# Finding the 24th candidate of a score row by folding sorted lists, for four tiles at once

## The chip, the cores and the metric

The kernel runs on one core of one Trainium2 chip. The metric is the device time of one execution in microseconds (us), median of three runs; the same program is profiled once more, and every instruction row below comes from that one profiled execution.

## The reference, cut to what matters

Top-32 attention, then a dense layer of three matmuls joined by a maximum, then a layer of eight experts of which each token goes to one. The part that the change touches is the attention (batch 4, 8 heads, 576 tokens, head size 64):

```
scores = scale * np.matmul(q, k.transpose(0, 1, 3, 2))
kth = np.partition(scores, -top_k, axis=-1)[..., -top_k:-top_k + 1]
mask = scores >= kth
scores = np.where(mask, scores, -1000000000.0)
scores = scores - np.max(scores, axis=-1, keepdims=True)
attn = np.exp(scores)
attn = attn / (np.sum(attn, axis=-1, keepdims=True) + 1e-09)
return np.matmul(attn, v).astype(np.float32)
```

Here `top_k` is 32. For every row of 576 scores the kernel must find the 32nd largest.

## The kernel before, in words

**Tiles.** The 4 x 8 x 576 rows of scores are cut into 144 tiles of 128 rows (`tiles`, `NTL`); a row has 576 scores. Four tiles in a row make a group (`G`), so there are 36 groups. The remainder of 64 rows of a head shares a tile with that of another head: four such "pair" tiles, one group, for each of the four batches.

**One loop of steps, a software pipeline.** The main loop counts steps `t`. In step `t` each stage works on the tile that lies its lag behind: scores of tile t+2 (TensorE), their copy out of PSUM for t+1 (`st_evac`, ScalarE), the search for tile t, and so on. The constants `L_...` are these lags. The order of the calls in the loop is the order of the instructions on each engine; there is no other scheduler. `bulk` is a list of VectorE pieces of the step and `tail_bulk` of pieces for its end; `run_bulk` issues them one by one and after each piece lets every open `chain` (a list of small instructions) issue one. Chains in `must` are issued to their end after `run_bulk`. `after(n, f)` puts work of other engines n steps later.

**The search, before.** `st_chunks` cuts the row of 576 into six pieces of 96 and takes the eight largest of each (MAX8 gives them sorted, largest first): 48 candidates. One step later `st_rounds` takes the eight largest of the 48, replaces them by a very low value (MATCH_REPLACE8, with a load of the eight values ahead of it), takes the next eight, replaces, and takes the third eight: the last of them is the 24th candidate. This is done for each tile by itself. `st_thr` (ScalarE) makes from it, tile by tile, the bound `bf`, and once a group the bias `be` of the later exponential from the largest value. `st_over` (ScalarE, lag 2) counts by the sign how many scores lie above the bound and marks them; `st_rest` (GpSimd, lag 3) subtracts the mark, which takes the marked ones out of the race; `st_next8` (VectorE, lag 4) takes the eight largest of what is left; `st_pick` makes a selector from the count, and `st_kth` (lag 8 of the group's first tile, ahead of the step's other VectorE work) picks the 32nd largest. From lag 9 on it is used: for two tiles of a group VectorE multiplies the exponential by a comparison (`st_mask`), for the other two ScalarE and GpSimd push the scores down ahead of the exponential (`st_gap`, `st_drop`). Then come splitting into two halves of 16 bit (`st_split`, `st_split2`), a transposing DMA (`st_ptr`) and the product with v (`st_av`), and `st_x` writes the group's result and turns it for the dense layer. `f` has two buffers (`NFB`), the marks `g` four (`NGB`).

**Other work in the same steps.** The matmuls of the dense layer and of the first experts run as units between the attention's (`run_units`), paced by a credit per step; weights are loaded and split into two halves of 16 bit (`prep_w`, `piece`). A last stretch without attention holds the rest of the experts.

**VectorE's PSUM bank.** One PSUM tile `vec` of 512 floats holds small operands of VectorE (`part` gives out pieces of it), among them the searches' results `vy8`.

**A second program.** `attempt(ctx, True)` is a slow exact version that runs only if the count `again` at the end says that the fast one missed a row; `general` marks its branches.

Of the kernel before, what the change touches and what calls it, by code (L numbers as in the profile page):

```python
# [12 lines left out]
ALU = mybir.AluOpType  # L13
# [6 lines left out]
def kernel(  # L20
# [74 lines left out]
    def attempt(ctx, general):  # L95
        const = ctx.enter_context(tc.tile_pool(name="const", bufs=1))
        iota32 = const.tile([P, G, 9], F32, name="iota32")
# [11 lines left out]
        NY8 = 3  # L109
# [12 lines left out]
        vy8 = [part(G * 9).rearrange("p (g e) -> p g e", g=G) for _ in range(NY8)]  # L122
        vt1 = [part(NE) for _ in range(3)]
# [7 lines left out]
        def consts():  # L131
# [8 lines left out]
            nc.vector.tensor_copy(out=viota, in_=iota32)  # L140
            nc.vector.tensor_copy(out=vrev, in_=rev8)
# [480 lines left out]
        with ExitStack() as p1:  # L622
# [26 lines left out]
            NPH, NHS = L_PTR - L_SPLIT + 1, 2  # L649
            phl = [a_p.tile([P, 2, SPAD], F16, name=f"phl{i}") for i in range(NPH)]  # L650
            if not general:

                hsel = a_p.tile([P, NHS, G, 9], F16, name="hsel")
                hkth = a_p.tile([P, NG, G], F32, name="hkth")
                heq = a_p.tile([P, NG, G, 1], F16, name="heq")
# [224 lines left out]
            Sps, Ss, T1, T3, zz, bf, be, cnt, y8, kth, ff, ee, pt = ({} for _ in range(13))  # L880
# [21 lines left out]
            cands, gg = {}, {}  # L902

            def st_chunks(n):
                if general:
                    return
                s = Ss[n]
                c = sm_p.tile([P, CAND * 8], F32, tag="c", name="c", bufs=2)
                cands[n] = c
                for j in range(0, CAND, 2):  # L910
                    def pair(j=j):
                        for i in (j, j + 1):
                            nc.vector.max(out=c[:, i * 8:(i + 1) * 8], in_=s[:, i * CW:(i + 1) * CW])  # L913
                    bulk.append(pair)

            def st_rounds(n):
                g, i = divmod(n, G)
                if i == 0:
                    T1[g] = sm_p.tile([P, G, 8], F32, tag="T1", name="T1", bufs=2)
                    if not general:  # L920
                        T3[g] = sm_p.tile([P, G, 8], F32, tag="T3", name="T3", bufs=2)
                if general:
                    return chain([lambda: nc.vector.max(out=T1[g][:, i], in_=Ss[n])])
                c = cands.pop(n)
                c2 = sm_p.tile([P, CAND * 8], F32, tag="c2", name="c2", bufs=1)
                t2 = sm_p.tile([P, 8], F32, tag="t2", name="t2", bufs=1)
# [9 lines left out]
            def st_bias(g):  # L936
                be[g] = sm_p.tile([P, G, 1], F32, tag="be", name="be")
                nc.scalar.activation(out=be[g], in_=T1[g][:, :, 0:1], func=ACTF.Copy, scale=-ESC)

            def st_thr(n):  # L940
                g, i = divmod(n, G)
                if general:
                    if i == G - 1:
                        st_bias(g)
                    return
                if i == 0:
                    cnt[g] = sm_p.tile([P, G, 1], F32, tag="cnt", name="cnt")
                    bf[g] = sm_p.tile([P, G, 1], F32, tag="bf", name="bf")
                nc.scalar.activation(out=bf[g][:, i], in_=T3[g][:, i, 7:8], func=ACTF.Copy, scale=-(1.0 - 2.0 ** -21))
                if i == G - 1:  # L950
                    st_bias(g)
# [15 lines left out]
            def st_next8(n):  # L967
# [3 lines left out]
                if i == 0:  # L971
                    y8[g] = vy8[g % NY8]
# [3 lines left out]
            def st_pick(g):  # L976
# [3 lines left out]
                bulk.append(lambda: nc.vector.tensor_tensor(out=hsel[:, g % NHS], in0=viota,  # L980
                                                            in1=cnt[g].to_broadcast([P, G, 9]), op=ALU.is_equal))
                tail_bulk.append(lambda: nc.vector.tensor_copy(out=y8[g][:, :, 0:1], in_=T3[g][:, :, 7:8]))
# [3 lines left out]
            def st_kth(g):  # L986
                kt = sm_p.tile([P, G], F32, tag="kth", name="kth") if general else hkth[:, g]
                kth[g] = kt
                if general:
# [13 lines left out]
                    lambda: nc.vector.tensor_tensor(out=y8[g], in0=hsel[:, g % NHS], in1=y8[g], op=ALU.mult),  # L1003
# [3 lines left out]
            def st_verdict():  # L1007

                hit = a_p.tile([P, NG * G], F16, name="hit")
# [71 lines left out]
            def st_x(g):  # L1081
# [6 lines left out]
                if first:  # L1088
# [3 lines left out]
                if kind == "pair":  # L1092
# [11 lines left out]
                def turn():  # L1104
# [4 lines left out]
                    else:  # L1109
                        if b % 2 == 0:  # L1110
                            xrem[b // 2] = m_ps[0].tile([P, 2, KD, 2 * REM], F16, tag="xR", name="xR", bufs=1)
                        xr = xrem[b // 2]
                        o = (b % 2) * REM
                        for i in range(2):
                            nc.sync.dma_start_transpose(
                                out=xr[:, i, :, o:o + REM],
                                in_=t[i * REM:(i + 1) * REM].rearrange("p e d -> p (e d)"),
                            )
                        if b % 2 == 1:
                            KH = KD // 2  # L1120
# [637 lines left out]
```

## Time and profile before

| what | us |
|---|---|
| median of 3 runs | 954.28 |
| lowest and highest | 954.03, 956.29 |
| the profiled execution, its own time | 951.46 |
| span of its instructions, first to last | 949.7 |
| VectorE (DVE) busy in it | 762.5 (80%) |
| TensorE (PE) busy | 751.6 (79%) |
| ScalarE (ACT) busy | 694.3 (73%) |
| GpSimd (POOL) busy | 608.6 (64%) |

A share of busy time is an average over the whole span. The attention lasts from about 23 us (the first copy of scores) to about 711 us (the last mask), and the engines' shares in it differ from those after it. The duration of an instruction in a row is from its start to its end; a following instruction of the same engine can start before that end, so what an instruction takes from its engine is better read from one start to the next.

### The profile page before, as it was taken

How to read it: one execution, taken by the hardware profiler on the slowest of the kernel's cores; microseconds unless marked ns; L12 is line 12 of the kernel's file. 1: busy time of each engine (PE TensorE's matmuls, PEld its weight loads, DVE VectorE, ACT ScalarE, POOL GpSimd, SP SyncE). 2: the span in 40 equal slices, each digit the busy share in tenths (PEclk: the TensorE clock that was granted, in tenths of full speed). 3: DMA queues.
4: the chain of work that ended last, by engine and by line, in shares of the span. 5: the costliest groups of instructions: out<-in, count | busy, mean ns of one | idle time of the engine just before them, and what ended most of it. 6: DMA issues, size and time to landing. Idle time of an engine off the chain costs nothing. (4 is left out here: it accounts for less than half of the span.)

```text
span 949.7 us, 29065 instructions
## 1 busy us (share of the span) xinstructions
PE 751.6 (79%) x10606; PEld 578.1 (61%) x10606; DVE 762.5 (80%) x3110; ACT 694.3 (73%) x1463; POOL 608.6 (64%) x552
## 2 busy tenths in 40 slices
PE   0212368888777899878898998889999999999992
PEld 0100237666555677657677787567887767588881
DVE  4999999999998999998998899788972335567671
ACT  2668899997898988898897997887863231466661
POOL 1457798998988789787877898687985221111110
PEclk9999999999998999899989999889999999999996
DMA  9681977775996788699969888687799358699270
GB/s 229 204 260 29 223 158 153 138 143 105 184 165 151 143 161 175 111 206 176 173 128 179 170 139 154 131 188 127 170 168 156 91 150 278 177 299 279 63 216 16
DMA packets 372164, 155.93 MB, mean 164 GB/s; under 512 B 331931, under 2 KB 348319, under 8 KB 372000
## 3 DMA queue, kind: packets, MB, share of 16 engines
q1 hardware_dynamic: 368128, 143.10, 71.9%
q0 software_dynamic: 3136, 9.46, 2.8%
q8 instruction: 87, 1.43, 0.6%
q10 hardware_dynamic: 736, 1.32, 0.5%
q14 instruction: 77, 0.63, 0.3%
HBM read 76.06 MB, written 16.67 MB: 98 GB/s over the span
## 5 line engine op out<-in xcount | busy, mean ns | idle before, releaser
L355 PEld LDWEIGHTS <-W 128*128 128x128 f16 x4560 | 248.2, 100 | 28.0 <-issue 25.2
L965 POOL TENSOR_TENSOR f<-s,g 128x576 f32<-128x576 f32 x144 | 200.9, 1395 | 69.6 <-DVE vec L974 32.9
L355 PE MATMUL mm<-xT,W 128*128 128x128 f16 x3456 | 210.5, 222 | 18.2 <-DVE W1h L741 6.8
L1058 POOL TENSOR_TENSOR phl<-e,phl 128x576 f16<-128x576 f32 x144 | 186.3, 1293 | 8.1 <-ACT phl L1054 7.9
L913 DVE MAX8 c<-s 128x8 f32<-128x96 f32 x864 | 175.2, 243 | 8.3 <-ACT s L899 4.7
L892 PEld LDWEIGHTS <-qT 128*128 128x128 f16 (+1 forms) x640 | 56.3, 108 | 188.9 <-issue 156.6
L892 PE MATMUL S<-kt,qT 128*128 128x64 f16 (+3 forms) x320 | 62.4, 345 | 109.9 <-ACT s L899 94.4
L1077 PE MATMUL av<-vh,pt 128*128 128x65 f16 (+3 forms) x1600 | 112.4, 201 | 17.4 <-DVE xn L1126 12.9
L1043 ACT ACTIVATE e<-s,be 128x576 f32<-128x576 f32 x144 | 110.6, 768 | 7.7 <-POOL phl L1058 5.7
L974 DVE MAX8 vec<-f 128x8 f32<-128x576 f32 x144 | 108.8, 755 | 5.3 <-POOL f L965 1.4
L959 ACT ACTIVATE g<-s,bf 128x576 uint16<-128x576 f32 x144 | 111.1, 771 | 0.1
L1048 DVE SCALAR_TENSOR_TENSOR e<-s,hkth,e 128x576 f32<-128x576 f32 x72 | 104.1, 1446 | 8.3 <-ACT e L1043 8.1
L1077 PEld LDWEIGHTS <-pt 128*128 128x128 f16 (+3 forms) x2400 | 90.8, 104 | 30.5 <-issue 17.6
L1054 ACT ACTIVATE phl<-e 128x576 f16<-128x576 f32 x144 | 97.4, 676 | 11.3 <-DMA pt<-phl 11.3
L899 ACT ACTIVATE s<-S 128x576 f32<-128x576 f32 x144 | 92.3, 641 | 15.5 <-PE S L892 14.6
L1077 PE MATMUL av<-vl,pt 128*128 128x64 f16 (+3 forms) x800 | 101.6, 199 | 0.0
L1037 POOL TENSOR_TENSOR s<-s,g 128x576 f32<-128x576 f32 x72 | 95.9, 1331 | 0.3
L456 DVE SCALAR_TENSOR_TENSOR W<-st,W 128x1024 f16<-128x1024 f32 x56 | 65.8, 1220 | 36.7 <-ACT W L455 34.6
L892 PE MATMUL S<-kT,qT 128*128 128x512 f16 (+3 forms) x320 | 48.5, 293 | 18.7 <-ACT s L899 18.7
L455 ACT ACTIVATE W<-st 128x1024 f16<-128x1024 f32 x56 | 55.6, 1046 | 1.8 <-DMA st<-in_moe_w_dram 1.8
L1034 ACT ACTIVATE g<-s,hkth 128x576 uint16<-128x576 f32 x72 | 55.4, 769 | 0.0
L1161 POOL TENSOR_TENSOR hhl<-a,hhl 128x384 f16<-128x384 f32 x36 | 34.7, 964 | 28.9 <-ACT hhl L1160 28.9
(232 smaller groups left out, 1586.4 us busy)
## 6 DMA issues: line engine op xcount, KB each, us to landing
st<-in_moe_w_dram SPq DMA_DIRECT2D x72, 512.0 KB
st<-in_moe_w_dram SPq DMA_DIRECT2D x28, 256.0 KB
raw<-in_moe_w_dram SPq DMA_DIRECT2D x12, 512.0 KB
st<-in_v_dram SPq DMA_DIRECT2D x16, 256.0 KB
hs<-he SPq DMA_DIRECT2D x16, 256.0 KB
hTe<-hs SPq DMA_DIRECT2D x8, 512.0 KB
st<-in_q_dram SPq DMA_DIRECT2D x15, 256.0 KB
qT<-qT SPq DMA_DIRECT2D x30, 128.0 KB
```

The lines of the kernel that those rows point to most:

```text
L355: nc.tensor.matmul(out=ps[:, o * n:(o + 1) * n], lhsT=w(b, kk, c), rhs=x(a, kk), start=(kk == 0 and i == 0), stop=(kk == KD - 1 and i == 2))
L892: nc.tensor.matmul(out=ps[o:o + m, j, 0:(REM if j else NQ * P)], lhsT=qt[:, vv, hh, 0:m], rhs=kr[:, hh] if j else km[:, hh // HG, :, hh % HG],
L913: nc.vector.max(out=c[:, i * 8:(i + 1) * 8], in_=s[:, i * CW:(i + 1) * CW])
L959: nc.scalar.activation(out=gg[n], in_=Ss[n], func=ACTF.Sign, bias=bf[g][:, i], accum_out=cnt[g][:, i])
L965: nc.gpsimd.tensor_tensor(out=ff[n], in0=Ss[n], in1=gg.pop(n).bitcast(F16), op=ALU.subtract)
L974: bulk.append(lambda: nc.vector.max(out=y8[g][:, i, 1:9], in_=y))
L1037: nc.gpsimd.tensor_tensor(out=Ss[n], in0=Ss[n], in1=zz.pop(n).bitcast(F16), op=ALU.subtract)
L1043: nc.scalar.activation(out=e, in_=Ss.pop(n) if early(n) else Ss[n], func=ACTF.Exp, scale=ESC, bias=be[g][:, i])
L1048: nc.vector.scalar_tensor_tensor(out=e, in0=Ss.pop(n), scalar=kth[g][:, i:i + 1], in1=e, op0=ALU.is_ge, op1=ALU.mult)
L1054: nc.scalar.activation(out=ph[:, 0, 0:S], in_=p, func=ACTF.Copy)
L1058: nc.gpsimd.tensor_tensor(out=ph[:, 1, 0:S], in0=p, in1=ph[:, 0, 0:S], op=ALU.subtract)
L1077: nc.tensor.matmul(out=av[o:o + m, i, 0:n], lhsT=t[0:kk, p * NCH + c, o:o + m], rhs=v_rows(x, b, c, hh)[:, 0:n], start=(c == 0 and p == 0 ...
```

## The change

The 24th candidate is found for a whole group at once, and without replacing anything. The six sorted lists of eight of each tile are kept in two tiles, `cand[0]` and `cand[1]` (three lists of each of the four tiles, 96 values a row). A list of the one is compared element by element with a list of the other read backwards. The larger values of the 24 comparisons are 24 of the candidates, the smaller ones the other 24; to make the first set the 24 largest, its smallest values are to be exchanged against the largest of the second. So `st_top` searches the eight smallest of the larger ones (by their negatives, in `top`) and the eight largest of the smaller ones (`low`), and one minimum and one maximum over those two lists of eight (`few`, `low`) give the 24th value. One operand of each comparison of two tensors is a negated copy in PSUM (`vneg`, `vfew`). That is 16 VectorE instructions for a group, the last of which makes the bound `bf` of the four tiles; before it were 28 a group in `st_rounds` (20 and 8 loads of values), one copy in `st_pick`, and four ScalarE instructions for `bf`.

The order in the steps moves with it. `st_top` is issued from the step of the group's last tile on, behind its chunks. `st_over` has lag 4 in place of 2 and `st_rest` lag 5 in place of 3; for the first tile of a group `st_over` stands behind `st_split` in ScalarE's order. `st_next8` has lag 5 in place of 4, so that the search stands in the step of the difference that it reads. `st_kth` keeps lag 8 but is issued at the end of the step's VectorE work. All later lags are the same. The results of pair tiles of an even batch now wait in `xq`, and the four transposing DMAs for two batches are issued together, into the ring `xT` (two buffers) in place of the tile `xR`. Small tiles are moved or shared (`iota32` lies in `top`, `hit` in PSUM).

```diff
-        NY8 = 3
+        NY8, CB = 3, CAND // 2 * 8
...
+        hit = part(NTL)
+        vneg = part(G * CB)
+        vfew = part(G * 8).rearrange("p (g e) -> p g e", g=G)
...
+        low = const.tile([P, G, 9], F32, name="low")
+        few = const.tile([P, G, 8], F32, name="few")
+        top = const.tile([P, G * CB], F32, name="top")
+        cand = [const.tile([P, G * CB], F32, name=f"cand{h}") for h in range(2)]
...
+            nc.vector.memset(low[:, :, 0:1], -LOW)
...
-        L_THR, L_OVER = 2, 2
+        L_OVER = G
         L_REST = L_OVER + 1
-        L_N8 = L_REST + 1
-        L_KTH = L_N8 + G - 1 + 1
-        L_EXP, L_MASK = L_KTH, L_KTH + 1
+        L_N8 = L_REST
+        L_KTH = L_N8 + G - 1
+        L_MASK = L_KTH + 1
...
+            lists = lambda x: x.rearrange("p (g c e) -> p g c e", g=G, e=8)
...
-                        for i in (j, j + 1):
-                            nc.vector.max(out=c[:, i * 8:(i + 1) * 8], in_=s[:, i * CW:(i + 1) * CW])
+                        for x in (j, j + 1):
+                            h, o = divmod(x, CAND // 2)
+                            nc.vector.max(out=lists(cand[h])[:, i, (o - h) % (CAND // 2)], in_=s[:, x * CW:(x + 1) * CW])
...
-                    lambda: nc.vector.max(out=T1[g][:, i], in_=c),
-                    lambda: nc.vector.match_replace(out=c2, in_to_replace=T1[g][:, i], in_values=c, imm_value=LOW),
-                    lambda: nc.vector.max(out=t2, in_=c2),
-                    lambda: nc.vector.match_replace(out=c, in_to_replace=t2, in_values=c2, imm_value=LOW),
-                    lambda: nc.vector.max(out=T3[g][:, i], in_=c),
...
+            def st_top(g):
+
+                a, b = lists(cand[0]), lists(cand[1])[:, :, :, ::-1]
+                T1[g] = sm_p.tile([P, G, 1], F32, tag="T1", name="T1", bufs=2)
+                y8[g] = vy8[g % NY8]
+                bf[g] = sm_p.tile([P, G, 1], F32, tag="bf", name="bf")
+                ops = [
+                    lambda: nc.vector.tensor_scalar(out=vneg, in0=cand[0], scalar1=-1.0, scalar2=None, op0=ALU.mult),
+                    lambda: nc.vector.scalar_tensor_tensor(out=a, in0=lists(vneg), scalar=-1.0, in1=b,
+                                                           op0=ALU.mult, op1=ALU.min),
+                    lambda: nc.vector.scalar_tensor_tensor(out=lists(top), in0=b, scalar=-1.0, in1=lists(vneg),
+                                                           op0=ALU.mult, op1=ALU.min),
+                    lambda: nc.vector.tensor_reduce(out=T1[g], in_=lists(top)[:, :, :, 0], axis=AX.X, op=ALU.min),
+                ]
+                for i in range(G):
+                    ops.append(lambda i=i: nc.vector.max(out=low[:, i, 1:9], in_=cand[0][:, i * CB:(i + 1) * CB]))
+                for i in range(G):
+                    ops.append(lambda i=i: nc.vector.max(out=few[:, i], in_=top[:, i * CB:(i + 1) * CB]))
+                ops += [
+                    lambda: nc.vector.tensor_scalar(out=vfew, in0=few, scalar1=-1.0, scalar2=None, op0=ALU.mult),
+                    lambda: nc.vector.tensor_tensor(out=few, in0=vfew, in1=low[:, :, 0:8], op=ALU.min),
+                    lambda: nc.vector.tensor_reduce(out=y8[g][:, :, 0:1], in_=few, axis=AX.X, op=ALU.max),
+                    lambda: nc.vector.tensor_scalar(out=bf[g], in0=y8[g][:, :, 0:1], scalar1=-(1.0 - 2.0 ** -21),
+                                                    scalar2=None, op0=ALU.mult),
                 ]
                 return chain(ops)
...
-                nc.scalar.activation(out=bf[g][:, i], in_=T3[g][:, i, 7:8], func=ACTF.Copy, scale=-(1.0 - 2.0 ** -21))
...
-                tail_bulk.append(lambda: nc.vector.tensor_copy(out=y8[g][:, :, 0:1], in_=T3[g][:, :, 7:8]))
...
                         if b % 2 == 0:
-                            xrem[b // 2] = m_ps[0].tile([P, 2, KD, 2 * REM], F16, tag="xR", name="xR", bufs=1)
...
+                            xrem[b // 2] = t
+                            return
+                        xt = m_ps[0].tile([P, 2 * KD, P], F16, tag="xT", name="xT", bufs=2)
+                        xr = xt.rearrange("p (i k) n -> p i k n", i=2)
+                        for o, rows in ((0, xrem[b // 2]), (REM, t)):
+                            for i in range(2):
+                                nc.sync.dma_start_transpose(
...
                     must = []
-                    n = t - L_KTH
-                    if ok(n) and n % G == 0:
-                        must.append(st_kth(n // G))
-                    if ok(t - 1):
-                        must.append(st_rounds(t - 1))
...
                     if ok(t):
                         st_chunks(t)
+                        if not general and t % G == G - 1:
+                            bulk.append(lambda g=t // G: must.append(st_top(g)))
...
-                    n = t - L_OVER
-                    if ok(n):
-                        st_thr(n)
...
                     n = t - L_OVER
                     if ok(n):
-                        st_over(n)
+                        if n % G == 0:
+                            st_thr(n // G)
+                        else:
+                            st_over(n)
...
                     if ok(n):
                         st_split(n)
+                    n = t - L_OVER
+                    if ok(n) and n % G == 0:
+                        st_over(n)
...
+                    n = t - L_KTH
+                    if ok(n) and n % G == 0:
+                        must.append(st_kth(n // G))
                     for c in must:
                         finish(c)
```

## Rows read from the trace of the kernel before

**Rows 1.** Page of the profile, part 1, whole run:

```profile
PE 751.6 (79%) x10606; PEld 578.1 (61%) x10606; DVE 762.5 (80%) x3110; ACT 694.3 (73%) x1463; POOL 608.6 (64%) x552
```

**Rows 2.** Busy us (instructions) by stretch: PE, PEld, DVE, ACT, POOL; then clock, DMA share, GB/s:

```profile
25.00:300.00 275.00, 166.42 (x2058) 117.14 (x2058) 266.62 (x1149) 234.62 (x527) 222.68 (x186) 0.98 0.74 159
300.00:500.00 200.00, 172.10 (x2555) 138.95 (x2554) 187.75 (x864) 176.02 (x395) 165.38 (x139) 0.93 0.82 159
500.00:700.00 200.00, 180.60 (x2819) 148.66 (x2816) 173.29 (x799) 166.87 (x374) 163.33 (x141) 0.95 0.83 159
700.00:925.00 225.00, 222.55 (x3107) 167.79 (x3104) 119.83 (x272) 106.27 (x157) 52.30 (x59) 1.00 0.71 188
```

**Rows 3.** Timeline of VectorE: start, duration, engine, line, operation:

```profile
401.10 0.20 DVE L928 MAX8 T<-c 128x8 f32<-128x48 f32 x1
401.22 0.40 DVE L913 MAX8 c<-s 128x8 f32<-128x96 f32 x2
401.54 0.18 DVE L1004 TENSOR_REDUCE hkth<-vec 128x4 f32<-128x36 f32 x1
401.63 0.08 DVE L929 MATCH_VALUE_LOAD c<-T,c 128x8 f32 x1
401.70 0.20 DVE L929 MATCH_REPLACE8 c<-T,c 128x48 f32<-128x48 f32 x1
401.81 0.41 DVE L913 MAX8 c<-s 128x8 f32<-128x96 f32 x2
...
402.25 0.75 DVE L974 MAX8 vec<-f 128x8 f32<-128x576 f32 x1
```

**Rows 4.** Groups by line and shape, VectorE, whole run:

```profile
L1048 DVE SCALAR_TENSOR_TENSOR e<-s,hkth,e 128x576 f32<-128x576 f32 x72 | 104.1, 1446 | 8.3 <-ACT e L1043 8.1
...
L1155 DVE TENSOR_TENSOR a<-a,mm 128x384 f32<-128x384 f32 x72 | 39.0, 542 | 15.9 <-PE mm L355 13.7 <-ACT xhl L1098 1.6
...
L982 DVE COPY vec<-T 128x4 f32<-128x4 f32 x36 | 5.6, 156 | 0.1
```

**Rows 5.** Timeline of VectorE, two instructions of which one needs the other:

```profile
415.26 0.16 DVE L1265 TENSOR_TENSOR base<-base,mm 128x8 f32<-128x8 f32 x1
415.45 0.15 DVE L1251 TENSOR_TENSOR snap<-base,vec 1x8 f32<-1x8 f32 x1
```

**Rows 6.** Groups by line and shape, ScalarE, whole run:

```profile
L949 ACT ACTIVATE bf<-T 128x1 f32<-128x1 f32 x144 | 28.1, 195 | 13.9 <-DVE T L932 13.9
```

**Rows 7.** Timeline of GpSimd, the differences f of five steps:

```profile
401.98 1.29 POOL L965 TENSOR_TENSOR f<-s,g 128x576 f32<-128x576 f32 x1
...
404.46 1.28 POOL L965 TENSOR_TENSOR f<-s,g 128x576 f32<-128x576 f32 x1
...
407.81 1.78 POOL L965 TENSOR_TENSOR f<-s,g 128x576 f32<-128x576 f32 x1 [0.16 <-ACT g L959]
...
413.28 1.80 POOL L965 TENSOR_TENSOR f<-s,g 128x576 f32<-128x576 f32 x1
...
418.15 1.73 POOL L965 TENSOR_TENSOR f<-s,g 128x576 f32<-128x576 f32 x1
```

**Rows 8.** Timeline of VectorE, the searches of eight after those differences:

```profile
405.67 0.77 DVE L974 MAX8 vec<-f 128x8 f32<-128x576 f32 x1
...
411.31 0.75 DVE L974 MAX8 vec<-f 128x8 f32<-128x576 f32 x1
...
416.84 0.77 DVE L974 MAX8 vec<-f 128x8 f32<-128x576 f32 x1
...
420.95 0.75 DVE L974 MAX8 vec<-f 128x8 f32<-128x576 f32 x1
```

**Rows 9.** Waits, whole run: who waited for whom, us, times, longest:

```profile
POOL f L965 <- DVE vec L974: 32.9, 18, 3.7
```

**Rows 10.** Timeline of ScalarE, first reader of the new kth:

```profile
407.62 0.78 ACT L1034 ACTIVATE g<-s,hkth 128x576 uint16<-128x576 f32 x1
```

**Rows 11.** Instructions on tile xR: count, duration ns min/median/max, first and last start:

```profile
L1115 SPq DMA_TRANSPOSE xR<-xhl x8: 1177/1242/1635, 259.7 to 613.8; - x8
```

More of the change, by code (lines that the diff above doesn't have):

```diff
@@ L877, in prep_w @@
                 return go
-            Sps, Ss, T1, T3, zz, bf, be, cnt, y8, kth, ff, ee, pt = ({} for _ in range(13))
+            Sps, Ss, T1, zz, bf, be, cnt, y8, kth, ff, ee, pt = ({} for _ in range(12))
             xhl, xrem, avt = {}, {}, {}
@@ L919, in st_rounds @@
                     T1[g] = sm_p.tile([P, G, 8], F32, tag="T1", name="T1", bufs=2)
[L920 to L926, printed above, removed]
@@ L927, in st_rounds @@
-                ops = [
-                    lambda: nc.vector.max(out=T1[g][:, i], in_=c),
-                    lambda: nc.vector.match_replace(out=c2, in_to_replace=T1[g][:, i], in_values=c, imm_value=LOW),
-                    lambda: nc.vector.max(out=t2, in_=c2),
-                    lambda: nc.vector.match_replace(out=c, in_to_replace=t2, in_values=c2, imm_value=LOW),
-                    lambda: nc.vector.max(out=T3[g][:, i], in_=c),
+                return chain([lambda: nc.vector.max(out=T1[g][:, i], in_=Ss[n])])
@@ L933, in st_rounds, with st_thr @@
                 ]
                 return chain(ops)
-            def st_bias(g):
+            def st_thr(g):
+                if not general:
+                    cnt[g] = sm_p.tile([P, G, 1], F32, tag="cnt", name="cnt")
                 be[g] = sm_p.tile([P, G, 1], F32, tag="be", name="be")
[L938 to L948, printed above, removed]
-                nc.scalar.activation(out=bf[g][:, i], in_=T3[g][:, i, 7:8], func=ACTF.Copy, scale=-(1.0 - 2.0 ** -21))
-                if i == G - 1:
-                    st_bias(g)
+                nc.scalar.activation(out=be[g], in_=T1[g][:, :, 0:1], func=ACTF.Copy, scale=-ESC if general else ESC)
@@ L1007, in st_verdict @@
             def st_verdict():
-                hit = a_p.tile([P, NG * G], F16, name="hit")
                 chain([
@@ L1087, in st_x @@
                 first = kind == "pair" or h == 0
-                if first:
+                if kind == "pair" and b % 2 == 0:
+                    xhl[b, qb] = x_p.tile([P, 2, G * D], F16, tag="xq", name="xq", bufs=1)
+                elif first:
                     xhl[b, qb] = x_p.tile([P, 2, DM], F16, tag="xhl", name="xhl")
@@ L1091, in st_x @@
                 off = 0 if first else G * D
-                if kind == "pair":
+                if kind == "pair" and b % 2 == 1:
                     t = t.rearrange("p e d -> p (e d)")[:, 0:nw].rearrange("p (e d) -> p e d", e=2)
@@ L1110, in turn @@
                         if b % 2 == 0:
-                            xrem[b // 2] = m_ps[0].tile([P, 2, KD, 2 * REM], F16, tag="xR", name="xR", bufs=1)
[L1112 to L1120, printed above, removed]
-                            new_job(NQ * B + b // 2,
-                                    lambda hl, kk: xr[:, kk % 2, hl * KH + kk // 2, :])
+                            xrem[b // 2] = t
[5 more added lines that the diff above has]
+                                nc.sync.dma_start_transpose(
+                                    out=xr[:, i, :, o:o + REM],
+                                    in_=rows[i * REM:(i + 1) * REM].rearrange("p e d -> p (e d)"),
+                                )
+                        KH = KD // 2
+                        new_job(NQ * B + b // 2, lambda hl, kk: xr[:, kk % 2, hl * KH + kk // 2, :])
                 chain([
@@ L1651, in attempt @@
                     if wq:
-                        for f, a in wq[:2 if t < L_KTH - 2 else 1]:
+                        for f, a in wq[:2 if t < 6 else 1]:
                             wq.pop(0)
@@ L1702, in attempt @@
                         chain(pick(ranked[-1].snap, sm_p.tile([1, 8], F32, tag="m8s", name="m8s")))
-                    if t == NTL + L_KTH and not general:
+                    if t == NTL + L_KTH + 1 and not general:
                         st_verdict()
```

23 lines of the change are left out of this document (10 added, 13 removed).

## The prediction, made before the change was run

> **What bounds the kernel now.** First the page: over the whole span VectorE and TensorE look equally full, 80% and 79% [rows 1], and no engine seems to be the limit. The table by stretch says otherwise [rows 2]. From 25 to 300 us VectorE is busy 266.62 of 275 us (97%), from 300 to 500 187.75 of 200 (94%), from 500 to 700 173.29 (87%). ScalarE has 85, 88 and 83%, GpSimd 81, 83 and 82%. From 700 to 925 us, behind the attention, TensorE is busy 222.55 of 225. So there are two regimes: an attention of 36 groups in about 675 us, 18.8 us a group, in which VectorE sets the pace, alone at first and more and more with others; and a last stretch that TensorE sets, in which the change alters nothing. The chain that ended last is of no use here, since it covers the end alone. What VectorE saves in the attention brings the last stretch forward by as much, as far as nobody else fills the hole.
>
> **What is removed.** In the timeline of VectorE [rows 3] I read from one start to the next, since starts overlap ends. A search over 48 values starts at 401.10 and its follower at 401.22: 0.12 us, though its duration is 0.20. Two searches over 96 take 401.22 to 401.54, 0.16 each. The load of eight values takes 0.07 (401.63 to 401.70), the replacing 0.11 (to 401.81). A tile's rounds are three searches, two loads, two replacings: 0.36 + 0.14 + 0.22 = 0.72 us, a group's four times that, 2.88. The copy at L982 goes too, 0.16 by its duration [rows 4]. Removed: 3.04 us a group. ScalarE loses four instructions a group at L949, 195 ns each by duration [rows 6], at most 0.8 us of its 18.8; it had waited there for VectorE 13.9 us in all.
>
> **What is added.** None of the 16 instructions is in the trace. 48 values in 0.12 (0.11 for the replacing) and 96 in 0.16 make about 1.04 ns a value and 0.06 us fixed. So three passes over 96 values are 0.48, the small maximum over twelve 0.07, eight searches over 24 values 8 x 0.085 = 0.68, three passes over 32 values 0.285, the bound 0.065: 1.58 us if each starts as soon as the engine can take it. But six of them read what the instruction just ahead has written. How long such a pair takes: L1251 reads what L1265 wrote and starts 0.19 us behind its start, by 0.03 more than its duration of 0.16 [rows 5], where eight values would be 0.07 by the line above. So a wait costs 0.12 us, six cost 0.72, and the upper bound is 2.30. The chain issues one instruction behind each remaining piece of the step (the search of eight, two or three conversions), so its first two waits lie under other pieces; the four at the end (smallest eight, negation, minimum, maximum, bound) are issued back to back. I take 1.58 + 0.48 = 2.06. `st_kth` was between other pieces and now ends the step, two instructions of which the second waits: 0.12 more. Saved: 3.04 - 2.06 - 0.12 = 0.86 us a group, 31 us in 36 groups; by the bounds 0.62 (22 us, every wait exposed) to 1.46 (53 us, none).
>
> The operand in PSUM decides whether this holds. The mask, with both operands in SBUF, takes 1446 ns in the mean for 576 values, twice what 1.04 ns a value gives; L1155, with one operand in PSUM, takes 542 for 384, which is 400 and some 140 fixed, what a search over 48 has beyond its 50 [rows 3, 4]. The new comparisons are of the second sort, so I give them no surcharge. The Trainium skill (VectorE: DVE Perf Modes, the section on the TRN2 errata) speaks against the change here: it puts the fixed part of an instruction that reads PSUM at 120 cycles against 58 for SBUF. By that, three instructions a group would cost 65 ns more, an estimate of 7 us in all. L1155's row does not show it, so the sum stays.
>
> **What is moved.** Ahead of ScalarE's `st_over` nothing new stands for three tiles of four. The first tile's waits for the end of the `st_top` chain, in the step before; it stands behind `st_evac` and `st_split`, so the next tile's scores are not behind it, but the step's last GpSimd work and the next step's are. `st_kth` lands later by most of a step. In the trace it ended about 401.7 and its first reader on ScalarE started at 407.62 [rows 3, 10], and a step is 4.7 us; some 2 us or more are left, so nothing for that. If they are gone, ScalarE stands with its evacuations behind. The pair tiles issue as many transposes, but four in one step of SP's queue: 1.24 us each [rows 11], so in two places 2.5 us more ahead of the attention's own transposes, whose product comes two steps later: nothing. The ring of two could make SP wait for a free buffer; the two pair jobs are far apart, and I cost that at nothing too.
>
> The one move that I do cost is `st_next8`. VectorE now searches `f` in the very step in which GpSimd writes it. In five steps of the trace GpSimd's difference ends at 403.27, 405.74, 409.59, 415.08, 419.88 [rows 7], and VectorE's search of that step (of the tile before) starts at 402.25, 405.67, 411.31, 416.84, 420.95 [rows 3, 8]. Today's order would thus be late by 1.02 and 0.07 us in two steps and early by 1.1 to 1.8 in three: 0.22 us a step, 31 us over 144. I take a fifth of it, 6 us. One reason: a wait is paid once, for a VectorE that has waited is later against GpSimd in the next step too. The other: GpSimd now sits 32.9 us in 18 waits for a free `f` [rows 9]. The search that frees it stood one step ahead of the difference and will stand two steps ahead.
>
> **The sum.** An even share of the groups is 14.7, 10.7 and 10.7 in the three stretches, so 12.6, 9.2 and 9.2 us of the 31. I let the first pass whole (VectorE at 97%), three quarters of the second and half of the third, where others hold the end more often: 12.6 + 6.9 + 4.6 = 24. Less 6: 18 us. The profiled execution took 951.46 us, 1.8 beyond its span, and is 2.8 below the median of the runs; 951.46 - 18 = 933.5, and 936 on the median's scale. Its own range, by the bounds of the added part and of the share that passes: 922 to 946.
>
> **The rivals.** A difference within 0.3%, 3 us, can't be told from none here.
> *Slower: the search waits in every step.* If GpSimd stays as late as today against VectorE, the whole 31 us are paid against 24: +7, 961. For it: GpSimd is at 82% and its passes are drawn out, 1.73 to 1.80 in three of the five rows [rows 7]. Against it: the two reasons above. It decides from 24 / 144 = 0.17 us a step. Chance 0.16.
> *No change: the threshold comes in a lump.* The step of the group's last tile now carries 2.06 us where each carried 0.72, and the first `st_over` of the next waits for all of it. If ScalarE is level with VectorE, each group pays up to that difference of 1.3 us; at half of it, 0.67 x 36 = 24, the gain is gone: 954. For it: ScalarE's 13.9 us of waits at L949 today [rows 6]. Against it: the place behind `st_split`. Chance 0.11.
> *Another engine takes over.* Only the first stretch gains: 12.6 - 6 = 7, 948. For it: ScalarE's 88 and 83%. Against it: ScalarE gets lighter too. Chance 0.15.
> *More than forecast.* If each instruction cost its full duration, as removed (0.20, 0.08 and 0.20 a piece, 4.8 us a group) so added (about 0.085 more for each of 16, 2.94), 1.86 a group or 67 us would be saved, by the same shares 52, less 6: 908. The Trainium skill says that of VectorE (VectorE: DVE Perf Modes, The DRAIN you can't avoid): the next instruction starts only when the pipe is empty. The starts 0.12 apart at 0.20 duration contradict it [rows 3]. Chance 0.06.
> *Forecast* as summed: 0.52.
> The search finds the same 24th value as before, so I see no way in which the second, slow program would start to run.
>
> **Chances and range.** Faster: forecast, takeover and more, 0.73; same 0.11; slower 0.16. The range leaves out the largest gain (0.06) and the upper half of the slower case (0.08), and a little of the forecast's edge: 918 to 958.
>
> **What would show it.** Right: the group of 16 at 2.0 to 2.1 us from first to last start less the pieces between; the 96-value passes near 0.24 in duration; VectorE's busy time down by about 31 us; the last mask some 18 us earlier than 711; 700 to 925 unchanged but shifted. Wrong: idle time of VectorE at the search of eight for GpSimd's `f` far above 6 us, ScalarE idle at the first `st_over` of each group, the reversed or PSUM operands at more than 0.3 us a pass, or VectorE less busy with the mask at the same time as before, which would mean that it never set the pace.

## The result, and the profile after

The changed kernel takes 960.37 us (median of five runs, 959.97 to 961.89) against 954.28 in the same job: a ratio of 1.0057, with a 95% interval of 1.0033 to 1.0081. It is slower by half a per cent, 6 us, where 18 us less were forecast. Several jobs ran, and the kernel before had medians from 954.2 to 958.9 in them, so below the ratio within a job is what compares, and microseconds worked out from it are on a scale of 954.

The page of the kernel after, its busy time by engine as in [rows 1], answers the first question: did VectorE get the relief?

```profile
PE 751.6 (78%) x10606; PEld 583.5 (61%) x10606; DVE 740.0 (77%) x2643; ACT 684.0 (71%) x1320; POOL 608.2 (63%) x552
```

It did: 467 instructions and 22.5 us less than the 762.5 of before. ScalarE lost 10.3. The table by stretch of the kernel after, columns as in [rows 2]:

```profile
25.00:300.00 275.00, 167.93 (x2105) 120.49 (x2105) 258.21 (x956) 230.60 (x466) 222.92 (x186) 0.94 0.76 157
300.00:500.00 200.00, 164.90 (x2405) 136.00 (x2403) 172.04 (x678) 164.35 (x334) 154.39 (x133) 0.91 0.85 154
500.00:700.00 200.00, 179.94 (x2808) 147.47 (x2806) 166.83 (x701) 166.20 (x340) 165.59 (x142) 0.97 0.86 156
```

None of the five engines is fuller than before by more than about 1% of a stretch. VectorE fell from 97, 94 and 87% to 94, 86 and 83%, and nobody used the room. Two lines of the groups and waits of the kernel after say what VectorE does in its new idle time. Two more have the masks, of the kernel after and then of the kernel before, with shortest, median and longest duration in ns and first and last start; the last start tells when the attention ends:

```profile
L983 DVE MAX8 vec<-f 128x8 f32<-128x576 f32 x144 | 109.8, 762 | 34.4 <-POOL f L976 29.5
```
```profile
POOL f L976 <- ACT g L970: 66.0, 41, 5.0
```
```profile
L1054 DVE SCALAR_TENSOR_TENSOR e<-s,hkth,e x72: 794/1142/6737, 76.4 to 719.9; 128x576 f32<-128x576 f32 x72
```
```profile
L1048 DVE SCALAR_TENSOR_TENSOR e<-s,hkth,e x72: 798/1054/7090, 78.0 to 710.9; 128x576 f32<-128x576 f32 x72
```

The search of eight now stands idle for 34.4 us, 29.5 of it for GpSimd's `f`, and GpSimd in turn waits 66.0 us for ScalarE's marks. In the kernel before GpSimd waited mostly the other way, for a buffer of `f` that the search had not yet freed [rows 9]. The last mask starts at 719.9 us; before it was 710.9. So the loss is in the attention, and the last stretch only follows.

The chain of one group in the timeline of VectorE after, from the negation (414.95) to the bound, with three pieces of other work between:

```profile
414.95 0.23 DVE L938 TENSOR_SCALAR vec<-cand 128x96 f32<-128x96 f32 x1
415.29 0.77 DVE L983 MAX8 vec<-f 128x8 f32<-128x576 f32 x1
416.10 0.26 DVE L939 SCALAR_TENSOR_TENSOR cand<-vec,cand 128x96 f32<-128x96 f32 x1
416.27 0.68 DVE L749 TENSOR_TENSOR hl<-mm,hl 128x512 f16<-128x512 f32 x1
416.87 0.24 DVE L941 SCALAR_TENSOR_TENSOR top<-cand,vec 128x96 f32<-128x96 f32 x1
417.03 0.55 DVE L1163 TENSOR_TENSOR a<-a,mm 128x384 f32<-128x384 f32 x1
417.49 0.17 DVE L943 TENSOR_REDUCE T<-top 128x4 f32<-128x12 f32 x1
417.58 0.43 DVE L946 MAX8 low<-cand 128x8 f32<-128x24 f32 x4
417.92 0.42 DVE L948 MAX8 few<-top 128x8 f32<-128x24 f32 x4
418.38 0.20 DVE L950 TENSOR_SCALAR vec<-few 128x32 f32<-128x32 f32 x1
418.61 0.19 DVE L951 TENSOR_TENSOR few<-vec,low 128x32 f32<-128x32 f32 x1
418.84 0.20 DVE L952 TENSOR_REDUCE vec<-few 128x4 f32<-128x32 f32 x1
419.06 0.16 DVE L953 TENSOR_SCALAR bf<-vec 128x4 f32<-128x4 f32 x1
419.14 0.25 DVE L922 MAX8 cand<-s 128x8 f32<-128x96 f32 x1
```

From start to next start, the other pieces left out, the sixteen take 0.34 + 0.17 + 0.16 + 0.09 + 0.34 + 0.46 + 0.23 + 0.23 + 0.22 + 0.08 = 2.32 us, where 2.06 were taken. The two passes with one operand in PSUM and the other read backwards are as cheap as hoped: 0.16 to 0.17 us, 0.24 to 0.26 in duration. At the end of the chain it is 0.23 us from one instruction to the next that needs it, and the sum had about 0.215 there (0.095 for 32 values and 0.12 for the wait). What it did not have is the 0.34 at the start: the search of eight behind the negation does not read it, yet starts only 0.10 us after the negation's end. In 24 of the 36 groups these two starts lie 0.33 to 0.36 us apart; in eleven others the search starts later still and the profile names GpSimd's `f`. Both instructions write the PSUM tile `vec`, which may be why the one waits for the other; that was not tested.

### The profile page after: what moved, and what is told of

Read it like the earlier page. It is cut to its first block, busy times and chain, and to the rows that moved or that the text cites. A ratio compares the mean times of both kernels' runs of the same rounds, so it can differ in the third digit from the quotient of the medians.

```text
span 959.7 us, 28507 instructions
## 1 busy us (share of the span) xinstructions
PE 751.6 (78%) x10606; PEld 583.5 (61%) x10606; DVE 740.0 (77%) x2643; ACT 684.0 (71%) x1320; POOL 608.2 (63%) x552
## 5 line engine op out<-in xcount | busy, mean ns | idle before, releaser
L363 PEld LDWEIGHTS <-W 128*128 128x128 f16 x4560 | 257.4, 102 | 35.0 <-issue 31.7
L363 PE MATMUL mm<-xT,W 128*128 128x128 f16 x3888 | 250.0, 228 | 29.3 <-DVE W1h L749 10.4
L976 POOL TENSOR_TENSOR f<-s,g 128x576 f32<-128x576 f32 x144 | 192.5, 1337 | 68.7 <-ACT g L970 66.0
L1064 POOL TENSOR_TENSOR phl<-e,phl 128x576 f16<-128x576 f32 x144 | 194.5, 1351 | 14.0 <-ACT phl L1060 13.7
L922 DVE MAX8 cand<-s 128x8 f32<-128x96 f32 x864 | 159.2, 241 | 2.0 <-ACT s L907 2.0
L983 DVE MAX8 vec<-f 128x8 f32<-128x576 f32 x144 | 109.8, 762 | 34.4 <-POOL f L976 29.5
L1054 DVE SCALAR_TENSOR_TENSOR e<-s,hkth,e 128x576 f32<-128x576 f32 x72 | 101.3, 1408 | 3.1 <-ACT e L1049 2.9
```

Of the source, the lines that this page charges most:

```text
L363: nc.tensor.matmul(out=ps[:, o * n:(o + 1) * n], lhsT=w(b, kk, c), rhs=x(a, kk), start=(kk == 0 and i == 0), stop=(kk == KD - 1 and i == 2))
L922: nc.vector.max(out=lists(cand[h])[:, i, (o - h) % (CAND // 2)], in_=s[:, x * CW:(x + 1) * CW])
L976: nc.gpsimd.tensor_tensor(out=ff[n], in0=Ss[n], in1=gg.pop(n).bitcast(F16), op=ALU.subtract)
L983: bulk.append(lambda: nc.vector.max(out=y8[g][:, i, 1:9], in_=y))
L1054: nc.vector.scalar_tensor_tensor(out=e, in0=Ss.pop(n), scalar=kth[g][:, i:i + 1], in1=e, op0=ALU.is_ge, op1=ALU.mult)
L1064: nc.gpsimd.tensor_tensor(out=ph[:, 1, 0:S], in0=p, in1=ph[:, 0, 0:S], op=ALU.subtract)
```

## The experiments

**1. VectorE relieved, nothing else changed.** In the kernel before, a tile's rounds end after the second search:

```diff
-                    lambda: nc.vector.max(out=t2, in_=c2),
-                    lambda: nc.vector.match_replace(out=c, in_to_replace=t2, in_values=c2, imm_value=LOW),
-                    lambda: nc.vector.max(out=T3[g][:, i], in_=c),
+                    lambda: nc.vector.max(out=T3[g][:, i], in_=c2),
```

> The kernel before, with its third round left out (no second replacing, no third search; the bound is then the 16th candidate in place of the 24th, the 32nd value is not found and the slow second program is switched off; every other instruction is issued as before). VectorE loses 0.30 us a tile by the starts in its timeline, 43 us in all. Theory pace (VectorE's work sets the attention's pace, as the prediction had it): by the prediction's shares 24/31 of it pass, about 33 us less, 921. Theory coupling (the pace is set by the chain of waits between the engines, and VectorE is only full because it is late in it): 945 to 954.

The whole run took longer, 1017.41 us (ratio 1.0639, 1.0606 to 1.0671), but that says nothing here: with other attention results the tokens go to other experts (the page has 10822 matmuls against 10606), and the last stretch had 322 us in place of 239. The attention can be read by itself, from the masks (first and last start) and the waits of this run:

```profile
L1045 DVE SCALAR_TENSOR_TENSOR e<-s,hkth,e x72: 795/1220/5105, 77.3 to 697.7; 128x576 f32<-128x576 f32 x72
```
```profile
DVE e L1045 <- ACT e L1040: 20.5, 18, 3.9
...
DVE c L913 <- ACT s L899: 9.7, 16, 1.6
```

The last mask starts at 697.7 against 710.9: 13 us for 43 of VectorE's work, 0.31 of it. VectorE now waits 20.5 us for ScalarE's exponential and 9.7 for the scores; before it was 8.1 and 4.7. The 13 us compare one execution with one. That of before was 2.8 us under its median and this one 4.2 over, so the share is an estimate, 0.31 to 0.47 (13 to 20 of 43). That lies between the two theories, above the 9 us at which the coupling theory's range ended and below the 33 of the other. VectorE's work passes on by a third to a half, and not by the three quarters of the sum.

**2. The search in the step of the difference, alone.** In the kernel before:

```diff
-        L_N8 = L_REST + 1
-        L_KTH = L_N8 + G - 1 + 1
+        L_N8 = L_REST
+        L_KTH = L_N8 + G + 1
```

> The kernel before, with one edit: the search of eight stands in the step of the difference that it reads, as in the changed kernel; all later lags stay. Theory wait (the search in the same step is what eats the gain): 8 to 20 us more, 962 to 974, with VectorE idle at the search for GpSimd's difference by 15 us or more. Theory lump (the threshold of four tiles at once, and the place of the first over pass, eat it): 954, within 3.

968.04 us, ratio 1.0125 (1.0093 to 1.0157): 12 us more. VectorE's own wait for `f` grows by 10, to 11.4, less than the 15 expected, and GpSimd's wait for the marks more than doubles from 22.5. The waits of this run, and the first of them in the kernel before:

```profile
POOL f L965 <- ACT g L959: 53.6, 49, 3.8
...
DVE vec L974 <- POOL f L965: 11.4, 15, 2.0
```
```profile
POOL f L965 <- ACT g L959: 22.5, 28, 2.2
```

**3 and 4. Two places in the changed kernel.** In the third run the first tile's over pass goes back to the place of the other three, in the fourth the search goes to the end of VectorE's step:

```diff
-                        if n % G == 0:
-                            st_thr(n // G)
-                        else:
-                            st_over(n)
+                        if n % G == 0:
+                            st_thr(n // G)
+                        st_over(n)
```
```diff
-                bulk.append(lambda: nc.vector.max(out=y8[g][:, i, 1:9], in_=y))
+                tail_bulk.append(lambda: nc.vector.max(out=y8[g][:, i, 1:9], in_=y))
```

> The changed kernel, with the over pass of a group's first tile at the place of the other three, ahead of the splitting and the gap pass on ScalarE. Theory lump (GpSimd waits 42 us for the first mark of a group since ScalarE makes it at the end of its step): 950 to 955, and GpSimd's wait at the first difference of a group falls under 20 us. Theory wait: 960, within 3.

> The changed kernel, with the search of eight among the last VectorE pieces of its step in place of behind the chunks, so that GpSimd has most of a step more for the difference. Theory wait: VectorE's idle time for the difference falls under 10 us and the time by 8 or more, to 952 or less. Theory lump: 960, within 3, since the mark still comes late.

The third: ratio 1.0082 (1.0048 to 1.0115), not better than the change. GpSimd's wait ahead of the first difference of a group fell from 42 to 23 us, and ScalarE now stands 15.9 us for the bound. The fourth: 1.0034 (1.0008 to 1.0060). VectorE's wait for `f` fell from 29.5 to 10.2 us but the time by 2 us only, within the intervals.

```profile
ACT g L970 <- DVE bf L953: 15.9, 18, 1.7
```
```profile
DVE vec L983 <- POOL f L976: 10.2, 14, 1.8
```

On the scale of 954 the third run has 962, which the wait theory named, and the fourth 957.5, which the lump theory named. So neither theory holds as it stood: the place of the over pass is not the cause, and a VectorE that waits less does not by itself finish earlier.

**5. The schedule without the folding.** The kernel before with its own rounds, in the lags and the order of the changed kernel:

```diff
-        L_THR, L_OVER = 2, 2
+        L_THR, L_OVER = 2, G
...
-        L_N8 = L_REST + 1
-        L_KTH = L_N8 + G - 1 + 1
+        L_N8 = L_REST
+        L_KTH = L_N8 + G - 1
```

with `st_kth` moved to the end of the step as in the change. The over pass of a group's first tile stays at the place of the other three, as in the third run.

> The kernel before with its rounds and its bounds tile by tile, but in the lags and the order of the changed kernel: over pass at lag 4, difference and search of eight both at lag 5, the 32nd value at the end of the step. Theory wait (the schedule costs about 12 us, as in the second experiment, and the folding gives some of it back): 964 to 970, above the changed kernel. Theory fold (the folding itself, in one lump a group, is what costs): 953 to 958.

962.51 us, ratio 1.0095 (1.0068 to 1.0122): 9 us for the schedule alone. Against the change's 1.0057 the folding then gives back some 4 us, and against the third run's 1.0082, which has the first over pass at the same place as this run, 1 us. These were measured in different jobs and all three intervals meet, so 1 to 4 is a size, not told from none. The time is below the expected 964 by little, and on the side of the wait theory.

**6, 7, 10 and 15. The search a step later again, in the changed kernel.** Each has `L_N8 = L_REST + 1`, and so every later lag one step longer; that needs one more score tile, and they differ in where its room comes from: three buffers for the marks (`NGB`, sixth run; the seventh has these without the later search), the normalized result `xn` in the marks' ring (tenth), or

```diff
-                    lambda: nc.vector.scalar_tensor_tensor(out=lists(top), in0=b, scalar=-1.0, in1=lists(vneg),
+                    lambda: nc.vector.scalar_tensor_tensor(out=b, in0=b, scalar=-1.0, in1=lists(vneg),
```

with four small tables of the last stretch laid over the lists (fifteenth).

> The changed kernel with the search of eight a step behind the difference again, every lag from there on one step longer, and three buffers for the marks in place of four to make room for the score tile that this keeps longer. Theory wait: the folding alone remains, 0.3 of some 25 us of VectorE's work, 945 to 950. Theory fold: 954 to 960.

> The changed kernel with three buffers for the marks in place of four, for comparison with the run that has the later search. Both theories: 960 to 963; what is above the changed kernel is the price of the buffer.

> The changed kernel with the search of eight a step behind the difference and every later lag one step longer, with all four buffers for the marks; the room comes from the attention's normalized result, which now takes a turn in the marks' ring in place of a tile of its own. Theory wait: the changed kernel less 9 us and the kernel before less 4: 948 to 952. If the longer lags or the ring cost as much as the folding gives: 954 to 957.

> The changed kernel with the search of eight a step behind the difference, all four marks' buffers and the normalized result in a tile of its own; the room comes from writing the second comparison over its own operand and from keeping four small tables of the last stretch where the lists were. Theory wait: the changed kernel less 9 us, the kernel before less 3 to 5: 949 to 952. If the one step longer lag costs by itself: 954 to 958.

Sixth: 1.0016 (0.9992 to 1.0040), within the folding theory's range; seventh: 1.0112 (1.0080 to 1.0143), above the 960 to 963 expected. With three marks the later search is worth 9 us, and the intervals are apart. Tenth: 1.0092 (1.0061 to 1.0124), above both of its ranges, and its waits show a new one: the result has to wait for GpSimd to read the mark whose buffer it takes.

```profile
DVE g L1135 <- POOL f L976: 12.2, 13, 2.4
```

Fifteenth: 1.0068 (1.0039 to 1.0098), also above both of its ranges and no better than the change, though its waits show the idle time for `f` gone, and some of it back at the mask:

```profile
DVE e L1053 <- ACT e L1048: 12.4, 10, 3.6
...
DVE vec L982 <- POOL f L975: 3.2, 2, 2.7
```

The sixth and the fifteenth do not agree: their intervals only touch, and what makes the 5 us between them is not settled. The sixth's trace can't tell, since its profiled execution was 4.8 us above its median and its last mask, at 719.1, is no earlier than the change's. What both say is that with most of the wait for `f` removed the changed kernel is not clearly faster than the kernel before.

**8 and 13. More VectorE work, spread and in a lump.** In the kernel before, one more replacing and one more search a tile (eighth), or the four pairs of a group at the end of its last tile's chain (thirteenth):

```diff
+                    lambda: nc.vector.match_replace(out=c2, in_to_replace=t2, in_values=c, imm_value=LOW),
+                    lambda: nc.vector.max(out=t2, in_=c2),
```

> The kernel before with 43 us more of VectorE work, 0.30 us a tile: one more replacing and one more search over 48 values, whose result nobody reads. Theory pace: VectorE is at 97 to 87% and has nowhere to put it, 30 to 43 us more, 985 to 998. Theory coupling (a third of VectorE's work shows in the time, as when 43 us were left out): 966 to 972.

> The kernel before with the same 43 us more of VectorE work as the eighth experiment, but not 0.30 us in every tile's chain: 1.2 us at the end of the chain of a group's last tile. Spread, it cost 18.6 us. Theory lump (a piece of VectorE's work costs more when it stands in one step of four, so the folding, which puts 2 us into one step, gives back less than its sum): 25 to 43 us more, 979 to 997. Theory even (where the work stands does not matter): 15 to 22 more, 969 to 976.

972.85 us against 954.23 (1.0199, 1.0170 to 1.0229) for the spread, 1007.88 against 954.40 (1.0547, 1.0510 to 1.0583) for the lump: 19 and 53 us. The spread is just above the coupling theory's 972, the lump above both of its ranges. But the lump is not the same work at another place. The pages of the two runs, spread first:

```profile
PE 754.7 (78%) x10606; PEld 583.0 (60%) x10606; DVE 795.1 (82%) x3542; ACT 696.1 (72%) x1463; POOL 608.6 (63%) x552
```
```profile
PE 763.4 (76%) x10606; PEld 590.1 (59%) x10606; DVE 831.7 (82%) x3542; ACT 697.5 (69%) x1463; POOL 611.7 (61%) x552
```

The same 3542 instructions cost VectorE 33 us more than before when spread and 69 in the lump. Some 15 of these 36 us are the masks, which were 104.1 us before [rows 4] and depend on GpSimd (last section); the groups of the two runs, spread first:

```profile
L1050 DVE SCALAR_TENSOR_TENSOR e<-s,hkth,e 128x576 f32<-128x576 f32 x72 | 96.3, 1338 | 6.0 <-ACT e L1045 6.0
```
```profile
L1054 DVE SCALAR_TENSOR_TENSOR e<-s,hkth,e 128x576 f32<-128x576 f32 x72 | 111.4, 1547 | 4.5 <-ACT e L1049 4.5
```

The timeline of the lump shows where the rest comes from:

```profile
419.23 0.07 DVE L937 MATCH_VALUE_LOAD c<-t,c 128x8 f32 x1
419.29 0.19 DVE L937 MATCH_REPLACE8 c<-t,c 128x48 f32<-128x48 f32 x1
419.52 0.21 DVE L938 MAX8 t<-c 128x8 f32<-128x48 f32 x1
419.76 0.09 DVE L937 MATCH_VALUE_LOAD c<-t,c 128x8 f32 x1
419.84 0.19 DVE L937 MATCH_REPLACE8 c<-t,c 128x48 f32<-128x48 f32 x1
```

With nothing between them a replacing and the search that reads it start 0.23 us apart, and a pair with its load is 0.53 to 0.56, where [rows 3] have 0.12, 0.07 and 0.11. Per microsecond that VectorE was busy more, the time grew by 0.57 (spread) and 0.77 (lump). Without the masks VectorE was busy 40 and 62 us more, and by that the figures are 0.46 and 0.86. How the 34 us between the two runs divide between the exposed waits and the place as such is not settled.

**9. The pair tiles alone.** The kernel before with `st_x` of the changed kernel.

> The kernel before with one part of the change alone: the results of an even batch's pair tiles wait and the four transposes for two batches are issued together, into the ring xT. The prediction costed this at nothing: 954, within 3. If it has a price, it is that of the part of the folding's gain that is missing, 3 to 6 us.

Ratio 1.0004 (0.9976 to 1.0032): nothing, as costed.

**11, 12 and 14. More work on the other engines.** In the kernel before, one edit each:

```diff
+                for x in range(2):
+                    nc.scalar.activation(out=junk, in_=Ss[n][:, x * 64:(x + 1) * 64], func=ACTF.Copy)
```
```diff
+                nc.gpsimd.tensor_tensor(out=junk, in0=Ss[n][:, 0:64], in1=Ss[n][:, 64:128], op=ALU.subtract)
```
```diff
+                for hh, o, m in hs:
+                    nc.tensor.matmul(out=ps[o:o + m, 0, 0:NQ * P], lhsT=qt[:, 0, hh, 0:m],
+                                     rhs=km[:, hh // HG, :, hh % HG], start=True, stop=True)
```

> The kernel before with two more ScalarE instructions a tile (copies of 64 values, right behind the over pass, that nobody reads), some 0.29 us a tile by the starts of its rows, 42 us in all. Theory coupling (every engine passes on a part of what it is given): 10 to 25 us more, 964 to 980. Theory ScalarE (it, not VectorE, sets the pace): 35 to 42 us more, 989 to 996.

> The kernel before with one more GpSimd instruction a tile (a difference of 64 values, right behind the difference f, that nobody reads), some 0.26 us a tile, 38 us in all. Theory coupling: 8 to 20 us more, 962 to 974. Theory GpSimd (it sets the pace, through the marks and f): 30 to 38 us more, 984 to 992. If it has room: 954 to 957.

> The kernel before with one more matmul of 512 columns a tile ahead of the scores (its result is overwritten by the scores), 0.2 to 0.5 us a tile by the rows of the scores' matmuls, 31 to 70 us in all. Theory TensorE (its order, scores behind the units, sets the pace that VectorE only follows): 30 us more or above, 984 or more. Theory VectorE first (it passes on 0.3 to 0.4 of its work, more than any other engine): less than 12 us more, under 966.

ScalarE, 52 us busier than before (746.5): ratio 1.0014 (0.9995 to 1.0034), not told from none, less than either theory had. GpSimd, 40 us busier (648.1): 1.0059 (1.0035 to 1.0084), 6 us, between no price and the coupling theory's 8 to 20. TensorE, 23 us busier (774.8): 0.9975 (0.9946 to 1.0004), none, as the theory with VectorE first had it. The table by stretch of ScalarE's run, columns as in [rows 2]:

```profile
25.00:300.00 275.00, 166.21 (x2054) 116.99 (x2054) 259.63 (x1146) 253.31 (x637) 220.88 (x185) 0.98 0.70 154
300.00:500.00 200.00, 170.42 (x2512) 138.67 (x2512) 179.27 (x844) 190.83 (x479) 162.76 (x138) 0.92 0.85 162
```

ScalarE is at 92 and 95% here, in the second stretch fuller than VectorE was before (94%), and the kernel is hardly slower.

## Why the prediction was wrong

**What VectorE saves: right in kind, at the lower edge of its bounds.** 0.86 us a group was the value, 0.62 to 1.46 the bounds, 22 to 53 us in all. By the starts of the group shown it is 3.04 - 2.32 - 0.12 = 0.60, 22 us. The page has 22.5, but 3 of these are the masks (104.1 before, 101.3 after), which the folding does not touch, so the close agreement is in part luck. The term that was too small is the start of the chain: 0.48 us were put down for the three passes over 96 values, with their waits hidden under other pieces, and they take 0.67, since the other piece behind the negation waits for it too. The waits at the end were priced almost rightly. The PSUM operands cost nothing extra, as the row said. By the Trainium skill (VectorE: DVE Perf Modes, the section on the TRN2 errata) they would have, and this trace does not bear it out: the two passes over 96 values that read PSUM took 243 and 255 ns in the mean against 241 for a search over 96 in SBUF.

**How much of it passes: the step that failed.** The sum let "the first pass whole (VectorE at 97%), three quarters of the second and half of the third", in all 24 of 31. Measured, 43 us taken from VectorE with nothing else touched shortened the attention by 13, at most some 20 (first run), and the folding's 22 us in the new order are worth 1 to 4 (fifth run against the third and the change). Some 20 of the 24 us between forecast and result are here: about 7 because VectorE saved 22 us and not 31, the rest because less of it passed. VectorE is the engine to whose work the time answers most, about 0.3 us for one taken away and 0.43 for one added (19 for 43 by the starts), against about 0.15 for GpSimd's 40 and none seen for ScalarE and TensorE. But relieved, it waits for ScalarE's exponential and scores a little later on. Why the share is so small is open beyond these waits.

**The wait at the search: right in place and too small.** 6 us were put down for it. Alone in the kernel before it costs 12; with the other moves of the schedule 9. The rival that ended slower was this one, and it decided in the end, though not at its price of 31 against 24: it took 9 against 1 to 4. It had a chance of 0.16.

**The signs.** Of the prediction's signs of being wrong two came: VectorE idle at the search of eight for `f` far above 6 us (29.5), and VectorE less busy with the masks no earlier. Two did not: no pass with a PSUM or reversed operand took 0.3 us, and in the trace of the change ScalarE does not stand idle ahead of the over passes; it is GpSimd that waits, for the marks that they write.

**The other rivals.** That the bounds come in a lump has some truth: the same instructions at the end of one step in four cost more (thirteenth run). But to give the first over pass its old place back did not help, so a late mark by that place was not the cause. Nothing was seen of the pair tiles' transposes. The largest gain, by full durations, was out: VectorE's busy time fell by 22.5 us and not by 67. TensorE's granted clock, which the forecast left out, is hardly the cause either. As a mean over the first two stretches it was 0.94 and 0.91 after against 0.98 and 0.93 before, mostly the upper of its two levels, 2.4 GHz; the ninth run had 0.94 and 0.93 and was no slower.

**The sum once more.** Schedule 9 us (0.95%), folding about -4: 5 to 6 us slower. This agrees with the measured time by construction, since the 4 is the difference of the two. Open is why the later search is worth 9 us with three buffers for the marks and nothing with four and the lists laid over; no version of the change that was tried beats the kernel before.

## What to carry to other kernels

A busy share of 97% does not mean that the time falls with that engine's work. Where several engines pass tiles around in short steps, measure the slope first: add some work that nobody reads to one engine, take some away, and look at the one stretch concerned. A saving that is bought by taking a step of slack out of the chain between engines has to pay for that slack, here 9 to 12 us for one step between a difference and its reader (second and fifth run, and the sixth against the seventh; the fifteenth did not get it back). And a chain of small dependent instructions is cheap only while other work stands between its links.

## What the runs showed of the hardware that had not been expected

A VectorE instruction with both operands in SBUF can stand for several GpSimd instructions, not one. The longest mask of the kernel after, in the timeline of VectorE, and what GpSimd does meanwhile:

```profile
212.54 6.74 DVE L1054 SCALAR_TENSOR_TENSOR e<-s,hkth,e 128x576 f32<-128x576 f32 x1
```
```profile
211.85 1.18 POOL L1265 DMA_INDIRECT xs<-xr,si  x1 [0.18 <-DVE cand L922]
213.06 1.29 POOL L1043 TENSOR_TENSOR s<-s,g 128x576 f32<-128x576 f32 x1
214.29 1.29 POOL L976 TENSOR_TENSOR f<-s,g 128x576 f32<-128x576 f32 x1
215.53 1.27 POOL L1064 TENSOR_TENSOR phl<-e,phl 128x576 f16<-128x576 f32 x1
216.77 0.66 POOL L1107 TENSOR_TENSOR xhl<-xn,xhl 128x256 f16<-128x256 f32 x1
217.39 1.26 POOL L1043 TENSOR_TENSOR s<-s,g 128x576 f32<-128x576 f32 x1
```

The mask lasts 6.74 us, where the shortest takes 0.79: it runs from 212.54 to 219.28, and ends 0.63 us after GpSimd's row of passes does (217.39 + 1.26 = 218.65), not much less than its own running time. It is not alone: all 53 masks of the kernel after that last over 0.82 us, and all 45 of the kernel before, end 0.61 to 0.63 us after the end of a GpSimd instruction, and the others take 0.79 to 0.81. This counts as busy: the 72 masks have 101 us after, and at 0.8 each they would have 58. So part of VectorE's 97% before was already a wait, for GpSimd, which may be one reason why its work passed on so little; that link was not tested. The Trainium skill (SBUF — State Buffer, SBUF: two separate sides) has the two engines hold a common port for a whole instruction, the other blocked; the trace agrees, and adds that the waiting one can be passed over by five passes in a row.
